# Float32 first-layer weights and x for two blocks, and float32 P and V turned by TensorE for the first

## The chip, the cores and the metric

One core of one Trainium2 chip runs the whole kernel. The metric is the device time of one execution in microseconds; a kernel is run several times and the median counts.

## What is computed

Attention over 4 batches, 8 heads, 576 positions and a head width of 64, with q and k rotated by position first, then two dense layers over the 2304 tokens that come out:

```python
q_rot, k_rot = (rotate(q), rotate(k))
scores = scale * np.matmul(q_rot, k_rot.transpose(0, 1, 3, 2))
attn = np.exp(scores - np.max(scores, axis=-1, keepdims=True))
attn = attn / (np.sum(attn, axis=-1, keepdims=True) + 1e-09)
x = np.matmul(attn, v)                     # to (2304, 512)
h = x @ w_in                               # (512, 2048)
g = np.maximum(h, 0.0) + alpha * np.minimum(h, 0.0)
out = g @ w_out                            # (2048, 512)
```

## The kernel before, in words

The tokens are 18 tiles of 128, two to a block, nine blocks. A batch has 4.5 tiles, so tiles 4 and 13 hold the end of one batch and the start of the next and are worked in halves (`half_pair`). Heads go in pairs: of each tile and pair of heads, `pair` has PE multiply q with k in float32 (L655; a half tile L683), and `head` then has DVE find the maximum (L707), ACT take the exponential with its sum (L716), ACT or DVE write 16 P as float16 (L721), DVE write what that leaves as a second float16 (L735), and SP turn both parts by one DMA transpose (L739). PE multiplies the turned parts with V (L746), which `values` holds as two float16 parts too; the low part of the first batch is made by PE (L467, L468) and copied by ACT (L471). After a tile's last pair `normalise` divides by the sums (y, L761), splits y into two float16 parts (L765 or L766, L768), and a DMA transpose makes x (xt, L775).

`expert` works a block's 16 slots, one for each 128 columns of w_in. The first layer is 12 float16 matmuls of 256 columns in two halves (L789: high by high, high by low, low by high), the activation is one ACT and one DVE instruction (L800, L803), and the second layer adds into a PSUM bank pair over all slots: for blocks 0 and 1 (`NF` = 2) as two float32 matmuls of 512 columns (L809), for the rest as six in a reduced float32 with g and w_out in two parts each (L827). `result` scales by a power of two on ACT (L839) and stores.

The weights come as raw float64 and are converted by three DVE instructions for each 128 x 512 chunk (`to_f32`, L508, L513, L517). `weights` does this for four groups, each of four chunks of w_in and four of w_out. For w_in ACT takes the absolute maximum (L538), a chain of small DVE instructions and one PE matmul makes a power-of-two scale (L542, L366 to L368, L354), and then ACT (L582) and DVE (L586) write two float16 parts; a w_out chunk is scaled by ACT (L599). `split` cuts w_out in two in block 1 for the blocks after it (L609, L613).

Block 0's attention runs first, alone, with the loads and the first weights. Then block 0's slots run beside block 1's attention and the other three groups of weights; block 1's slots run beside block 2's attention, and so on. The order on each engine's queue is written out ahead of time: every operation has a priority (`at`, the slot in which it is wanted, less a lead from `PRM`) and prices in ns for the engines that may take it, and `Plan.run` goes through a model of the five engines, giving a free engine its most urgent ready operation. On the chip each engine works through its queue in order. In the plan DVE and POOL share a port. Three PSUM bank pairs (`pair_T`) hold scores in block 0's attention; SP issues all loads, stores and transposes.

## Time and profile before

| | |
|---|---|
| median of 3 runs | 688.65 us (685.98 to 691.06) |
| profiled execution | 684.13 us |
| its span in the profile | 682.3 us |
| PE busy | 608.4 us, 89% |
| DVE busy | 507.9 us, 74% |
| ACT busy | 339.9 us, 50% |
| POOL busy | 181.0 us, 27% |

PE is TensorE's matmuls, PEld its weight loads, DVE VectorE, ACT ScalarE, POOL GpSimd, SP SyncE. Ends of matmuls are modelled in the profile, so a price of PE is best read from the start of one group to the start of the next. A float32 matmul stands in the trace as two instructions. The granted clock is a share of 2.4 GHz; 0.5 is 1.2 GHz.

### The profile page before, as it was taken

The page shows a single profiled execution, that of the slowest core. Times are in us where ns is not written, and L with a number is a line of the kernel's source. Part 1 is how long each engine was busy: PE and PEld are TensorE (multiplying, and loading weights), DVE is VectorE, ACT ScalarE, POOL GpSimd, SP SyncE. Part 2 cuts the span into 40 slices and gives each one's busy share as a digit, 9 for nine tenths or more (in the row PEclk, how much of TensorE's full clock was granted, in tenths as well). Part 3 has the DMA queues.
Part 4 walks back from the last instruction along what each step waited for, and adds up shares of the span by engine and source line. Part 5 has one row for each costly group of instructions (what it writes and reads, how often), then busy time and mean ns, then how long its engine had stood idle before and what let it go on. Part 6 is the DMA issues. An engine that isn't in the chain of part 4 may idle for free.

```text
span 682.3 us, 13828 instructions
## 1 busy us (share of the span) xinstructions
PE 608.4 (89%) x5384; PEld 443.8 (65%) x5384; DVE 507.9 (74%) x879; ACT 339.9 (50%) x766; POOL 181.0 (27%) x145
## 2 busy tenths in 40 slices
PE   0656678779899999999999999999999999999997
PEld 0334444455656567777767777677777777777775
DVE  5998999999778776768886586777866667765332
ACT  3536747539743435545654545464545445543322
POOL 4763000204642212126623222253211202110000
PEclk9966669979999999999999999999999999999999
DMA  8999898695985745468896456774445555462000
GB/s 302 312 233 226 159 292 214 193 272 121 222 167 108 135 86 132 86 114 184 198 211 106 99 118 103 112 183 100 84 69 105 110 78 86 101 119 54 32 0 32
DMA packets 209009, 96.47 MB, mean 141 GB/s; under 512 B 191792, under 2 KB 196016, under 8 KB 208944
## 3 DMA queue, kind: packets, MB, share of 16 engines
q1 hardware_dynamic: 208944, 95.59, 63.0%
q8 instruction: 42, 0.69, 0.4%
q14 instruction: 23, 0.19, 0.1%
HBM read 41.56 MB, written 4.72 MB: 68 GB/s over the span
## 4 chain that ended last, share of the span: by engine, by line
PE 68%; DMA 18%; DVE 10%; issue 1%; ACT 1%; SPq 1%; POOL 0%; ACTq 0%; DVEq 0%; POOLq 0%
PE h L789 24%; PE pair L827 21%; DMA pt<-pp 14%; PE v L746 8%; PE pair L655 8%; PE pair L809 5%; PE pair L683 2%; DVE kraw L390 1%; DMA qr<-in_q_dram 1%; DMA kraw<-in_k_dram 1%; DVE pp L735 1%; DVE mx L707 1%; DVE wi L586 1%; DMA wraw<-in_moe_w_out_dram 1%; DVE wraw L517 1%
## 5 line engine op out<-in xcount | busy, mean ns | idle before, releaser
L789 PE MATMUL h<-xt,wi 128*128 128x256 f16 x1728 | 231.4, 277 | 11.1 <-DVE r L803 10.6
L789 PEld LDWEIGHTS <-wi 128*128 128x128 f16 x1728 | 156.3, 99 | 72.3 <-issue 53.5
L716 ACT ACTIVATE e<-pair,mx 128x576 f32<-128x576 f32 x144 | 105.6, 736 | 87.7 <-DVE mx L707 83.5
L735 DVE SCALAR_TENSOR_TENSOR pp<-e,pp 128x576 f16<-128x576 f32 x144 | 126.1, 882 | 8.1 <-ACT pp L721 7.0
L803 DVE SCALAR_TENSOR_TENSOR r<-r,beta,h 128x256 f32<-128x256 f32 x144 | 68.7, 477 | 75.9 <-ACT r L800 75.6
L800 ACT ACTIVATE r<-h 128x256 f32<-128x256 f32 x144 | 55.1, 383 | 132.4 <-PE h L789 129.5
L746 PE MATMUL v<-vv,pt 128*128 128x64 f16 (+1 forms) x2240 | 92.6, 199 | 30.1 <-DMA pt<-pp 29.8
L746 PEld LDWEIGHTS <-pt 128*128 128x128 f16 (+1 forms) x2240 | 84.0, 104 | 51.3 <-DMA pt<-pp 41.6
L707 DVE TENSOR_REDUCE mx<-pair 128x1 f32<-128x576 f32 x144 | 103.2, 750 | 11.7 <-PE pair L655 10.3
L827 PE MATMUL pair<-wh,gh 128*128 128x512 f32 x224 | 96.0, 429 | 0.7 <-ACT gh L817 0.7
L655 PE MATMUL pair<-ks,qn 64*128 64x288 f32 x512 | 89.4, 453 | 7.2 <-ACT e L716 6.2
L827 PE MATMUL pair<-wh,gl 128*128 128x512 f32 x224 | 87.6, 391 | 0.8 <-POOL gl L820 0.8
L827 PE MATMUL pair<-wo,gh 128*128 128x512 f32 x224 | 88.2, 394 | 0.0
L820 POOL TENSOR_TENSOR gl<-r,gh 128x256 fp32r<-128x256 f32 x49 | 48.3, 986 | 116.5 <-ACT gh L817 80.1
L655 PEld LDWEIGHTS pair<-ks,qn 64*128 64x128 f32 x512 | 48.8, 196 | 35.5 <-issue 12.5
L721 ACT ACTIVATE pp<-e 128x576 f16<-128x576 f32 x90 | 61.1, 681 | 15.8 <-DMA pt<-pp 14.8
L817 ACT ACTIVATE gh<-r 128x256 fp32r<-128x256 f32 x97 | 40.4, 416 | 51.0 <-PE pair L827 33.9
L809 PE MATMUL pair<-wo,r 128*128 128x512 f32 x128 | 61.7, 607 | 0.0
L768 POOL TENSOR_TENSOR xs<-y,xs 128x512 f16<-128x512 f32 (+1 forms) x19 | 27.8, 1463 | 109.9 <-DVE xs L766 85.9
L827 PEld LDWEIGHTS pair<-wh,gl 128*128 128x128 f32 x224 | 42.0, 188 | 11.2 <-POOL gl L820 1.6
L827 PEld LDWEIGHTS pair<-wh,gh 128*128 128x128 f32 x224 | 42.2, 189 | 10.1 <-issue 1.9
L820 DVE TENSOR_TENSOR gl<-r,gh 128x256 fp32r<-128x256 f32 x63 | 28.7, 456 | 26.2 <-ACT gh L817 25.5
(77 smaller groups left out, 555.3 us busy)
## 6 DMA issues: line engine op xcount, KB each, us to landing
kraw<-in_k_dram SPq DMA_DIRECT2D x16, 576.0 KB, 4.6
qr<-in_q_dram SPq DMA_DIRECT2D x18, 512.0 KB, 4.2
wraw<-in_moe_w_in_dram SPq DMA_DIRECT2D x16, 512.0 KB, 5.5
wraw<-in_moe_w_out_dram SPq DMA_DIRECT2D x16, 512.0 KB, 5.6
vraw<-in_v_dram SPq DMA_DIRECT2D x16, 320.0 KB, 4.4
out_dram<-os SPq DMA_DIRECT2D x18, 256.0 KB, 2.2
pt<-pp SPq DMA_TRANSPOSE x144, 3.4
vv<-vv SPq DMA_DIRECT2D x32, 64.0 KB, 2.2
```

The source lines that it names most:

```text
L655: nc.tensor.matmul(out=ps[h]()[:, x, :HS], lhsT=qn()[r, p], rhs=kt()[r, x * HS:(x + 1) * HS], start=True, stop=True)
L707: lambda e: nc.vector.tensor_reduce(out=mx()[a:z], in_=ps()[a:z, :, :HS], axis=AX.XY, op=ALU.max, negate=True),
L716: lambda e: nc.scalar.activation(out=ex()[a:z].rearrange("p (x c) -> p x c", x=2), in_=ps()[a:z, :, :HS], func=ACTF.Exp, bias=mx()[a:z], a ...
L721: lambda e: nc.scalar.activation(out=pp()[a:z, 0], in_=ex()[a:z], func=ACTF.Copy, scale=1.0 if early else E_SC) if e == ACT
L735: lambda e: nc.vector.scalar_tensor_tensor(out=pp()[a:z, 1], in0=ex()[a:z], scalar=E_SC, in1=pp()[a:z, 0], op0=ALU.mult, op1=ALU.subtract),
L746: nc.tensor.matmul(out=v_b()[c:d, 2 * p + g], lhsT=pt()[:, s, o:o + d - c], rhs=vt()[:, g, w], start=(n == 0), stop=(n == len(order) - 1))
L789: nc.tensor.matmul(out=ps(), lhsT=wi_b()[:, kk, j // FG, w, f], rhs=x()[:, y * KC + kk], start=(kk == 0 and n == 0), stop=(kk == KC - 1 an ...
L800: lambda e: nc.scalar.activation(out=g(), in_=ps(), func=ACTF.Relu, scale=-1.0),
L803: lambda e: nc.vector.scalar_tensor_tensor(out=g(), in0=g(), scalar=beta_b()[:, j:j + 1], in1=ps(), op0=ALU.mult, op1=ALU.add),
L809: nc.tensor.matmul(out=po()[:, x], lhsT=g()[:, x * 128:(x + 1) * 128], rhs=wf[j](), start=(j == 0), stop=(j == KF - 1))
L820: lambda e: ENG[e].tensor_tensor(out=gl(), in0=g(), in1=gh().bitcast(F32), op=ALU.subtract),
L827: nc.tensor.matmul(out=po()[:, x], lhsT=s()[:, ts], rhs=w, start=(j == 0 and c == 0), stop=(j == KF - 1 and c == 2))
```

## The change

- `weights` only converts now, two chunks in one instruction (`load_two`, `to_f32` on 1024 elements), in place, and keeps the absolute maxima; w_in stands in SBUF as float32.
- Blocks 0 and 1 do the first layer with four float32 matmuls of 256 columns (`l1_f32`) on a float32 x, which `normalise` makes for tiles 0 to 3 by four matmuls of y against the identity and a copy out of PSUM.
- In block 1's slots one scale for all of w_in is made (`bound_w_in`), and after each group's last slot `split_in` writes the two float16 parts over the float32 ones, for blocks 2 to 8. w_out isn't scaled any more; `result` multiplies by the scale from block 2 on.
- For tiles 0 and 1, `head_f32` takes the place of the second half of `head`: five float32 matmuls of 128 columns of the exponentials against the identity, into the PSUM tile that held the scores, one copy to SBUF on ACT or DVE, and five float32 matmuls of 64 columns with the raw V. V's scale is multiplied into the reciprocal sums instead.
- `PRM`, the leads of all operations, has new values throughout; for instance keys lead by 23.6 and not 40.87, batch 0's V by 40.33 and not 32.45, units look ahead by 3 and not 2. Prices of the plan change: DVE's fixed part from 68 to 130 ns, a small DVE instruction from 75 to 150, the DMA rate from 360 to 340, two halves of the first layer for blocks 0 and 1 at 860 instead of 655.
- The attention of block 1 no longer interleaves with `weights` in program order, which matters only between equal priorities.

```diff
+    def load_two(at, g, src):
+        raw, token = wr_T.new(), flow.new()
+        for x in range(2):
+            op(at, {SP: t_dma(128 * 512 * 8)},
+               lambda e, x=x: nc.sync.dma_start(out=raw()[:, x].rearrange("p f w -> p (f w)").bitcast(I64), in_=src(x)),
+               writes=[(raw, x), token])
+        return raw, token
+
+    def w32(c, g):
+        return wi_b().bitcast(F32)[:, c, g].rearrange("p a b -> p (a b)")
 
     def weights(g):
         at = slot(0, FG * g)
-        wm, m, ps = wm_T.new(), column(at - 8), pair_T[1 + g % 2].new()
-        raws = []
+        for c in range(0, KC, 2):
+            raw, token = load_two(at - PRM["wl"] + PRM["wg"] * g, g, lambda x, c=c: w_in[c + x, g])
+            two = lambda c=c: wi_b().bitcast(F32)[:, c:c + 2, g].rearrange("p c a b -> p c (a b)")
+            ti, acc = lambda two=two: two().bitcast(I32), [(wi_b, (c, g)), (wi_b, (c + 1, g))]
+            to_f32(at - PRM["wb"], raw, ti, acc, ti, acc, token)
+            op(at - PRM["ws"], {ACT: t_act(1024, ap=1)},
+               lambda e, raw=raw, c=c, two=two: nc.scalar.activation(
+                   out=raw().bitcast(F32)[:, :, :, 1], in_=two(), func=ACTF.Abs, accum_out=wmax_b()[:, c // 2, g:g + 1]),
+               reads=acc, writes=[(raw, 0), (raw, 1), (wmax_b, (c, g))])
+        for n in range(g * FG // 2, (g + 1) * FG // 2):
+            w = new_wf(n)
+            wf[n] = w
+            at = slot(0, 2 * n)
+            raw, token = load_two(at - PRM["wl2"] + PRM["wg"] * g, g, lambda x, n=n: w_out[2 * n + x])
+            ti = lambda w=w: w().bitcast(I32)
+            to_f32(at - PRM["wb2"], raw, ti, [w], ti, [w], token)
...
+    def split_in(g):
+        at = slot(NF, FG * g) - PRM["si"]
         for c in range(KC):
-            raw, token = wr_T.new(), flow.new()
-            raws.append((raw, token))
-            op(at - PRM.get('wl', 16) + PRM.get('wg', 2) * g, {SP: t_dma(128 * 512 * 8)},
-               lambda e, raw=raw, c=c: nc.sync.dma_start(
-                   out=raw().rearrange("p f w -> p (f w)").bitcast(I64), in_=w_in[c, g]),
-               writes=[raw, token])
-        for c, (raw, token) in enumerate(raws):
-            tmp = lambda c=c: wi_b().bitcast(I32)[:, c, g]
-            dst = lambda raw=raw: raw()[:, :, 1]
-            to_f32(at - PRM.get('wb', 5), raw, tmp, (wi_b, (c, g)), dst, raw, token)
-            op(at - PRM.get('wb', 5), {ACT: t_act(512, ap=1)},
-               lambda e, raw=raw, c=c, tmp=tmp: nc.scalar.activation(
-                   out=tmp().bitcast(F32), in_=raw().bitcast(F32)[:, :, 1], func=ACTF.Abs,
-                   accum_out=wm()[:, c:c + 1]),
-               reads=[raw], writes=[(wi_b, (c, g)), (wm, c)])
-        op(at - 4, {DVE: 80}, lambda e: nc.vector.tensor_reduce(out=m()[:, 0:1], in_=wm(), axis=AX.X, op=ALU.max),
-           reads=[(wm, c) for c in range(KC)], writes=[m], port=False)
-        bound(at - 4, m, lambda: we_b()[:, g:g + 1], (we_b, g), ps)
-        we, wsc, wus = (lambda b=b: b()[:, g:g + 1] for b in (we_b, wsc_b, wus_b))
-        scale_of(at - 4, wsc, (wsc_b, g), we, (we_b, g))
-        small(at - 4, lambda: scalar(wus(), we(), 2.0**-14, None, ALU.mult), reads=[(we_b, g)], writes=[(wus_b, g)])
-        by_pe = g < PRM["wpe"]
-        if by_pe:
-            dg = diagonal(at - 4, wsc, (wsc_b, g))
-        for c, (raw, _) in enumerate(raws):
-            f = lambda raw=raw: raw().bitcast(F32)[:, :, 1]
-            t = lambda c=c: wi_b()[:, c, g]
-            acc = (wi_b, (c, g))
-            if by_pe:
-                op(at - PRM['ws'], {ACT: t_act(512, ap=1)},
-                   lambda e, f=f, t=t: nc.scalar.activation(
-                       out=t()[:, 0], in_=f(), func=ACTF.Copy, scale=wsc_b()[:, g:g + 1]),
-                   reads=[raw, (wsc_b, g)], writes=[acc])
-                if c % 2:
-                    ps = pair_T[1 + g % 2].new()
-                    last = raws[c - 1][0]
-                    low_part(at - PRM['ws'], dg, ps,
-                             lambda ps=ps, c=c, rs=(last, raw): [
-                                 (ps()[:, x], rs[x]().bitcast(F32)[:, :, 1], wi_b()[:, c - 1 + x, g, 0]) for x in range(2)],
-                             lambda ps=ps, c=c: (wi_b()[:, c - 1:c + 1, g, 1], ps()),
-                             [last, raw, (wi_b, (c - 1, g))], [(wi_b, (c - 1, g)), acc], 1024)
-                continue
-            if c >= PRM["fi"]:
-                op(at - PRM.get('ws', 3), {ACT: t_act(512, ap=1)},
-                   lambda e, f=f: nc.scalar.activation(out=f(), in_=f(), func=ACTF.Copy, scale=wsc_b()[:, g:g + 1]),
-                   reads=[(wsc_b, g)], writes=[raw])
-                op(at - PRM.get('ws', 3), {ACT: t_act(512), DVE: (t_dve(512, fast=True), PRM.get('wh', 4))},
-                   lambda e, f=f, t=t: nc.scalar.activation(out=t()[:, 0], in_=f(), func=ACTF.Copy) if e == ACT
-                   else nc.vector.tensor_copy(out=t()[:, 0], in_=f()),
-                   reads=[raw], writes=[acc])
-                op(at - PRM.get('ws', 3), {POOL: t_pool(512, True), DVE: (t_dve(512), PRM.get('wlo', 0))},
-                   lambda e, f=f, t=t: ENG[e].tensor_tensor(out=t()[:, 1], in0=f(), in1=t()[:, 0], op=ALU.subtract),
-                   reads=[raw], writes=[acc])
-                continue
-            op(at - PRM.get('ws', 3), {ACT: t_act(512, ap=1)},
-               lambda e, f=f, t=t: nc.scalar.activation(
-                   out=t()[:, 0], in_=f(), func=ACTF.Copy, scale=wsc_b()[:, g:g + 1]),
-               reads=[raw, (wsc_b, g)], writes=[acc])
-            op(at - PRM.get('ws', 3), {DVE: t_dve(512, 1)},
-               lambda e, f=f, t=t: nc.vector.scalar_tensor_tensor(
-                   out=t()[:, 1], in0=f(), scalar=wsc_b()[:, g:g + 1], in1=t()[:, 0], op0=ALU.mult, op1=ALU.subtract),
-               reads=[raw, (wsc_b, g)], writes=[acc])
-        for j in range(g * FG, (g + 1) * FG):
-            raw, token, w = wr_T.new(), flow.new(), new_wf(j)
-            wf[j] = w
-            at = slot(0, j)
-            op(at - PRM.get('wl2', 14) + PRM.get('wg', 2) * g, {SP: t_dma(128 * 512 * 8)},
-               lambda e, raw=raw, j=j: nc.sync.dma_start(out=raw().rearrange("p f w -> p (f w)").bitcast(I64), in_=w_out[j]),
-               writes=[raw, token])
-            ti = lambda w=w: w().bitcast(I32)
-            to_f32(at - PRM.get('wb2', 3), raw, ti, w, ti, w, token)
-            op(at - PRM['ws2'], {ACT: t_act(512, ap=1)},
-               lambda e, w=w: nc.scalar.activation(out=w(), in_=w(), func=ACTF.Copy, scale=wus_b()[:, g:g + 1]),
-               reads=[(wus_b, g)], writes=[w])
+            tmp, acc, t = os_T.new(), (wi_b, (c, g)), lambda c=c: wi_b()[:, c, g]
+            op(at, {ACT: t_act(512, ap=1), DVE: (t_dve(512, fast=True), PRM["sd"])},
+               lambda e, c=c, tmp=tmp: nc.scalar.activation(out=tmp(), in_=w32(c, g), func=ACTF.Copy, scale=wsc_b())
+               if e == ACT else scalar(tmp(), w32(c, g), wsc_b(), None, ALU.mult),
+               reads=[acc, wsc_b], writes=[tmp])
+            op(at, {ACT: t_act(512), DVE: (t_dve(512, fast=True), PRM["sd"])},
+               lambda e, t=t, tmp=tmp: nc.scalar.activation(out=t()[:, 0], in_=tmp(), func=ACTF.Copy) if e == ACT
+               else nc.vector.tensor_copy(out=t()[:, 0], in_=tmp()),
+               reads=[tmp], writes=[acc])
...
+            op(at, {POOL: t_pool(512, True), DVE: (t_dve(512), PRM["wlo"])},
+               lambda e, t=t, tmp=tmp: ENG[e].tensor_tensor(out=t()[:, 1], in0=tmp(), in1=t()[:, 0], op=ALU.subtract),
+               reads=[tmp], writes=[acc])
...
+        if t < PRM["pf"]:
+            return head_f32(at, t, b, p, h, ex, ps, pt)
+        pp = pp_T.new()
...
+    def head_f32(at, t, b, p, h, ex, ps, pt):
+        v_b, raw = vos[t], vraw[b, p]
+        pt.make = lambda: pt_T.pool.tile([128, NH, 128], F32, name="pt", tag=f"pt{pt_T.opened % pt_T.bufs}")
+        flat = lambda: ps().rearrange("p x c -> p (x c)")
+
+        def turn(e):
+            for s in range(NH):
+                w = min(128, S - 128 * s)
+                nc.tensor.matmul(out=flat()[:w, 128 * s:128 * s + 128], lhsT=ex()[:, 128 * s:128 * s + w],
+                                 rhs=eye_b(), start=True, stop=True)
+
+        def pv(e):
+            for s in range(NH):
+                w = min(128, S - 128 * s)
+                nc.tensor.matmul(out=v_b()[:, 2 * p + h], lhsT=pt()[:w, s], rhs=raw()[:w, h, s],
+                                 start=(s == 0), stop=(s == NH - 1))
+
+        op(at + 0.3, {PE: 1300}, turn, kind=WIDE, reads=[ex, eye_b], writes=[ps])
+        op(at + 0.3, {ACT: t_act(NH * 128, True), DVE: (t_dve(NH * 128), PRM["pc"])},
+           lambda e: nc.scalar.activation(out=pt().rearrange("p s c -> p (s c)"), in_=flat()[:, :NH * 128], func=ACTF.Copy) if e == ACT
+           else nc.vector.tensor_copy(out=pt().rearrange("p s c -> p (s c)"), in_=flat()[:, :NH * 128]),
+           reads=[ps], writes=[pt], port=False)
+        op(at + 0.6, {PE: 1000}, pv, kind=WIDE, reads=[pt, raw], writes=[(v_b, (2 * p + h, 0))])
...
+        if t < PRM["pf"]:
+            small(at, lambda: scalar(r(), r(), vs[b]()[a:z], None, ALU.mult), reads=[vs[b]], writes=[rs])
...
+        if t < 2 * NF:
+            i, o = divmod(t, 2)
+            if i not in xt:
+                xt[i] = xt_T.new()
+                xt[i].make = lambda: xt_T.pool.tile([128, KC, 256], F32, name="xt", tag=f"xt{xt_T.opened % xt_T.bufs}")
+            yf, vf = lambda: y().rearrange("p h d -> p (h d)"), lambda: vo().rearrange("p h d -> p (h d)")
+
+            def turn(e):
+                for c in range(KC):
+                    w = slice(128 * c, 128 * c + 128)
+                    nc.tensor.matmul(out=vf()[:, w], lhsT=yf()[:, w], rhs=eye_b(), start=True, stop=True)
+
+            op(at, {PE: 1100}, turn, kind=WIDE, reads=[(y, a), eye_b], writes=[(vo, (h, a)) for h in range(H)])
+            op(at, {ACT: t_act(DM, True), DVE: (t_dve(DM), 2)},
+               lambda e: (nc.scalar.copy if e == ACT else nc.vector.tensor_copy)(
+                   out=xt[i]()[:, :, o * 128:(o + 1) * 128], in_=vf().rearrange("p (c n) -> p c n", c=KC)),
+               reads=[(vo, (h, a)) for h in range(H)], writes=[(xt[i], o)], port=False)
+            return
...
+        def l1_f32(e, half):
+            f = slice(j % FG * 128, (j % FG + 1) * 128)
+            for kk in range(half * KC // 2, (half + 1) * KC // 2):
+                nc.tensor.matmul(out=ps(), lhsT=w32(kk, j // FG)[:, f], rhs=x()[:, kk], start=(kk == 0), stop=(kk == KC - 1))
...
-            op(at, {PE: 655}, lambda e, half=half: l1(e, half), kind=HALF * half,
+            op(at, {PE: 860 if i < NF else 655}, lambda e, half=half: (l1_f32 if i < NF else l1)(e, half), kind=HALF * half,
...
+                if j == 0:
+                    bound_w_in()
+                if j % FG == FG - 1 and j < KF - 1:
+                    split_in(j // FG)
         result(i, po)
+        if i == NF - 1:
```

## Rows read from the trace of the kernel before

**Rows 1.** The page's 40 slices of the span (17 us each), in tenths.
```profile
PE   0656678779899999999999999999999999999997
...
DVE  5998999999778776768886586777866667765332
...
PEclk9966669979999999999999999999999999999999
```

**Rows 2.** Windows by stage: busy us of each engine, granted clock, DMA share, GB/s.
```profile
core 0: us, PE busy (x) PEld busy (x) DVE busy (x) ACT busy (x) POOL busy (x), PEclk, DMA share, GB/s
20.00:85.20 65.20, 41.25 (x342) 26.48 (x340) 59.77 (x84) 37.45 (x77) 28.63 (x16) 0.69 0.95 228
85.20:184.10 98.90, 80.21 (x593) 49.02 (x593) 94.19 (x181) 63.17 (x135) 23.32 (x18) 0.89 0.82 214
184.10:262.00 77.90, 75.28 (x680) 48.91 (x679) 60.22 (x96) 33.42 (x73) 22.58 (x16) 1.00 0.62 128
```

**Rows 3.** The chain that ended last, stage A: start us, us, what.
```profile
31.64 7.67 DMA pt<-pp
...
42.57 7.55 DMA pt<-pp x2
...
53.09 5.07 DMA pt<-pp
...
60.66 9.33 DMA pt<-pp x2
```

**Rows 4.** PE's timeline, full clock: start us, us, line, operation, count.
```profile
152.18 0.28 PE L368 MATMUL pair<-cr,ones 128*128 128x1 f32 x2
152.32 0.57 PE L746 MATMUL v<-vv,pt 128*128 128x64 f16 x14
152.72 0.82 PE L789 MATMUL h<-xt,wi 128*128 128x256 f16 x6
153.47 1.24 PE L655 MATMUL pair<-ks,qn 64*128 64x288 f32 x8
154.65 0.83 PE L789 MATMUL h<-xt,wi 128*128 128x256 f16 x6
...
164.11 2.19 PE L683 MATMUL pair<-ks,qd 128*128 128x288 f32 x8
166.13 1.47 PE L789 MATMUL h<-xt,wi 128*128 128x256 f16 x12
167.44 1.88 PE L809 MATMUL pair<-wo,r 128*128 128x512 f32 x4
169.16 0.57 PE L746 MATMUL v<-vv,pt 128*128 128x64 f16 x14
```

**Rows 5.** Groups by line, whole span, then PE in stage A: busy us, mean ns.
```profile
L683 PEld LDWEIGHTS pair<-ks,qd 128*128 128x128 f32 x64 | 11.6, 190 | 3.3 <-issue 0.7 <-ACT xs L765 0.2
...
L471 ACT ACTIVATE vv<-pair 128x640 f16<-128x640 f32 x4 | 2.8, 703 | 5.9 <-PE pair L468 5.9
...
L467 PE MATMUL pair<-vraw,dg 128*128 128x320 f32 x14 | 5.7, 499 | 1.6 <-ACT vv L471 1.6
```

**Rows 6.** DVE's groups by line in stage A, the last in stage M0.
```profile
L735 DVE SCALAR_TENSOR_TENSOR pp<-e,pp 128x576 f16<-128x576 f32 x18 | 17.2, 963 | 2.3 <-ACT pp L721 2.3
...
L354 DVE TENSOR_SCALAR pp<-e 128x576 f16<-128x576 f32 x2 | 4.7, 2348 | 0.7 <-DMA pt<-pp 0.7
...
L586 DVE SCALAR_TENSOR_TENSOR wi<-wraw,wsc,wi 128x512 f16<-128x512 f32 x4 | 3.7, 965 | 0.0
...
L354 DVE TENSOR_SCALAR wus<-we 128x1 f32<-128x1 f32 x1 | 0.1, 142 | 0.0
...
L586 DVE SCALAR_TENSOR_TENSOR wi<-wraw,wsc,wi 128x512 f16<-128x512 f32 x13 | 10.5, 818 | 0.0
```

**Rows 7.** Timelines of DVE and PE between block 0's last y and its first slot.
```profile
78.67 0.68 DVE L761 TENSOR_TENSOR y<-v,rs 128x512 f32<-128x512 f32 x1
...
85.17 2.72 PE L789 MATMUL h<-xt,wi 128*128 128x256 f16 x12 [0.23 <-DMA xt<-xs]
```

More of the change, by code (lines that the diff above doesn't have):

```diff
@@ L617, in attention_moe @@
+           reads=[f, (h, j % 4)], writes=[(l, y)])
     qs = {}
@@ L907, in attention_moe @@
         result(i, po[i])
+    if NF == NB:
+        raise ValueError("the second block comes with float32 weights")
     for i in range(NB, len(blocks)):
```

157 lines of the change are left out of this document (86 added, 71 removed).

## The prediction

> **What bounds the kernel now.** I read the page's slices first [rows 1]: from about 190 us on PE is in its highest tenth and at full clock in nearly every slice, so what is left to win there is work, not waiting; before that PE is mostly at six to eight tenths, while DVE stands at nine. Next the stages [rows 2], cut where the PE timeline shows block 0's attention, block 0's expert layers and block 1's expert layers to begin and end. From 20 to 85.2 us (call it A: block 0's attention, first weights) DVE is busy 59.8 of 65.2 us, the DMA engines 95%, PE only 41.3 us and at a granted clock of 0.69, so part of that is half speed (1.2 and not 2.4 GHz). From 85.2 to 184.1 us (M0: block 0's 16 slots, block 1's attention, three quarters of the weights) DVE is busy 94.2 of 98.9 us, PE 80.2 at 0.89. From 184.1 to 262 us (M1: block 1's slots) PE is busy 75.3 of 77.9 at 1.00 and DVE 60.2. A and M0 are bound by DVE and, in A, by transposes; M1 and all that follows by PE. The chain of A says which wait ends last there [rows 3]: four pieces of it, 29.6 us together, are six DMA transposes of P, 4.9 us each with the queue before them, and PE sits idle until they land.
>
> **The change part by part.** All PE prices are start to start at full clock, from one stretch [rows 4]: QK of a pair 1.18 us (153.47 to 154.65), P times V of one head in float16 0.40 (14 matmuls, 152.32 to 152.72), the first layer of a slot in float16 1.31 (166.13 to 167.44), the second in float32 1.72 (167.44 to 169.16).
>
> *First layer in float32, 32 slots.* 12 float16 matmuls of 256 columns become 4 float32 ones of 256. The second layer has 2 float32 matmuls of 512, the same number of columns, at 1.72; so the first costs 1.72 and not 1.31, 0.41 more, 6.6 us for each of the two blocks. M1 is PE's already, so there it is paid in full; in M0 it is paid only if PE has become the bound.
>
> *P in float32, 16 heads.* A head loses the float16 copy, DVE's subtraction and a DMA transpose with SP's issue, and gains on PE 5 float32 matmuls of 128 columns (P against the identity), a copy of 640 elements out of PSUM, and 5 float32 matmuls of 64 columns (P times V). The trace writes a float32 matmul as two instructions. The one of 288 columns takes 2.02 us for 8 (164.11 to 166.13 in [rows 4]), 253 ns, 0.88 ns a column; so the turning is 10 x 112 ns = 1.12 us. For 64 columns that price would be 56 ns, but a weight load goes with each: the one-column matmul with its float32 load, twice, keeps PE 0.14 us (152.18 to 152.32 in [rows 4]), 70 ns each. So P times V is 0.70, a head 1.82 instead of 0.40, and 16 heads 29.1 instead of 6.4: 22.7 us more. Bounds: by columns alone a head is 1.68 (2.2 us less in all); if each of the 20 loads held PE for its whole 190 ns [rows 5] it would be 3.8 (31.7 us more). I take 1.82, because in [rows 4] the loads of equal kind hide behind their matmuls.
>
> The Trainium skill (TensorE: Matmul & The Clock Gate, sections LDWEIGHTS (loading the stationary operand) and Weight-path perf modes) speaks against this: a load costs the stationary operand's columns over 1.2 in ns, 107 for 128, and the fast load is not to be had with float32. By it, as an estimate, P times V would be 10 x 107 ns, a head 2.2 us and the 16 heads 6 us dearer than my sum, which rival (b) covers; the trace's 70 ns for load and matmul together is under that.
>
> The copy out of PSUM goes to ACT or DVE; a 640 wide one on ACT takes 0.70 us [rows 5], what the float16 copy of P took there, so ACT gains nothing and loses nothing. DVE loses in A the subtraction, 16 of the 18 for 17.2 us, 15.3, and the two copies it made for 4.7 [rows 6].
>
> *x in float32, 4 tiles.* Split, subtraction on POOL and transpose go; 4 float32 matmuls of 128 columns (8 x 112 ns, 0.9 us) and a copy of 512 come. From y to the first layer it took 6.5 us (78.67 to 85.17) [rows 7]; now about 0.7 + 0.9 + 0.7 and the handovers, some 2.5. Four microseconds less at the start of M0, 3.6 us more PE over both blocks.
>
> *Weights.* Group by group, w_in is no longer scaled and split before block 0's first layer: the subtractions of L586, 3.7 us of DVE in A and 10.5 in M0, go, and so do the bound and scale chains, about a dozen small instructions a group, 1 us in A and 3 in M0. Converting 1024 at a time makes 48 instructions of 96; what that saves no row shows by itself, and it lies between nothing and 48 times the 0.14 us of a whole one-column instruction [rows 6], 7 us. I take 3 over A and M0, 2.5 of it in M0. The scaling of w_out on ACT goes into the last copy, for nothing. The split of w_in comes back in M1: 16 times two copies and a subtraction, about 1.3 us ACT (or less on DVE) and 1.5 us POOL each. In M1 ACT is busy 33.4 and POOL 22.6 of 77.9 us [rows 2], which covers 21 and 24 us. If it did not, block 2's first slots would be late by what is missing, at most a few us; its bound needs one PE matmul with a DVE chain of under 1 us.
>
> *SP and DMA.* 16 transposes of P and 4 of x leave SP's queue; the loads behind them (L530, L594, q) go out earlier. The loads keep their bytes. V is loaded ahead of K now; the first QK waits for K and q in either order, so I leave 20 us as the start.
>
> *The sum.* A after: V's low part some 5 us of PE at full clock (its float32 half in A is 5.7 us busy, partly cold [rows 5], and the float16 half beside it is smaller), QK 8 x 1.18 = 9.4, heads 29.1, two turns of x 1.8: 45 us. DVE's is 59.8 - 15.3 - 4.7 - 3.7 - 1 = 35. PE is now the longer of the two. What clock? In A, PE was cold with idle gaps from P's transposes in its queue; those gaps go, the work per pair triples, and at half clock PE would have no idle time at all, the condition in which the trace shows 1.00 (M1). So I take full clock. PSUM lets little more than one pair be in flight: QK, maximum, exponential, turning, copy of a first head are 1.2 + 0.75 + 0.75 + 1.1 + 0.7 and four handovers, about 5.4 us, against 4.8 of PE work in a pair. That is 85 to 88%. So A takes 45 / 0.85 = 53 us, and M0 starts at about 75 and not 85.2. M0 after: 16 x (1.72 + 1.72) = 55, six QK 7.1, half pairs 4.9, P times V 8, two turns 1.8, and two pairs of block 1 that stood in A before, 3.2: 80 us. DVE: 94.2 - 10.5 - 3 - 2.5 and 5 for those pairs, 83. Two engines near 80 leave neither free; at the 95% that DVE had, 88 us. M0 ends at 163 and not 184.1: 21 us won. M1 gives 6.6 back. Net 14.5: the profiled execution (span 682.3, 684.1 with what lies around it) becomes about 669.6, 2.1% less, and the median of the runs, 688.65, about 674.
>
> **Rivals.** (a) *The gain is whole*: A and M0 dense on PE at 95%, 125 us from 20, M0 ends at 152; net 25, 663. For it speaks that M1 runs at 97%; against it that DVE needs 83 us in M0 by itself. (b) *Nothing comes of it*: the heads cost 2.3 us (the planner's own prices in the diff, 1300 and 1000), 8 us more, and PE, whose queue is in order, waits at each turning for an exponential that DVE's conversions have delayed, so A keeps its end near 83. Then M0 ends at 171 to 177 and net it is 0 to 7: 682 to 689. For it speaks that DVE's instructions in A are drawn out beside a busy POOL (963 ns for a subtraction, 2348 for a copy of P [rows 6]) and might stay so. (c) *Slower*: the clock stays low in A. 45 us of PE work at 0.5 with no gap are 90, so M0 starts at 110 and ends near 198, net 21 the other way, 709. It decides from a granted clock under some 0.6 in A; there the 0.69 of before would give 45 / 0.69 / 0.85 = 77, M0 from 99 and a loss of about 10, 699. For it speaks only that A was cold; against it that it was cold beside idle PE. (d) That the split of w_in doesn't fit beside M1 is a mishap of a few us within (b).
>
> **How the numbers follow.** About 1% (7 us) is what a measurement of this kernel can tell from no change. The forecast, 7 to 21 us won, has 0.48, its own range 667 to 682; (a) 0.15; (b) 0.21; (c) 0.16. So faster 0.63, within 1% 0.21, slower 0.16. The range reaches from (a) with cheap heads, 655, to the milder half of (c) and the dear heads, 697; beyond it lie the rest of (c) and a little of (a).
>
> **What would show it.** In the changed profile: no P transposes ahead of M0; granted clock in A near 1; first-layer float32 slots at 1.72 us; a turning of 10 instructions at 1.1 and P times V at 0.7; first L1 of block 0 near 75 us and block 0's last second layer near 163; M1 about 6 us longer than 77.9 at 1.00; DVE in A well under nine tenths. Wrong if: the clock of A stays near 0.69, loads make the heads 3 us, PE's gaps wait for DVE or ACT before turnings, or the later, PE-bound part (from 262 us on), which I leave at its length, moves by more than 3 us through the new priorities.

## The result and the profile after

The changed kernel takes 678.33 us in the median of 4 runs (675.64 to 680.75), the kernel before 689.38 beside it (4 runs). The ratio is 0.9851, 95% interval 0.9818 to 0.9883: 1.5% faster, 10 to 11 us. The prediction said 674.0, range 655 to 697, and the forecast's own range 667 to 682 holds the median. The profiled run took 676.41 us, span 674.6, against 684.13 and 682.3. The time is right; the way there is not the one predicted. Stage times come from the one traced execution of each kernel, which for `b_pf2`, `b_newprm`, `a_pad`, `a_l1h1` and `o_late` is the slowest of its runs and for `a_l1h0` the fastest. Cut at block 0's first slot and at the ends of the two blocks' second layers, as in [rows 2] (the last column is the time behind 262 us before, behind 253.1 us after):

| | A ends at | M0 | M1 | behind M1 |
|---|---|---|---|---|
| before | 85.2 | 98.9 | 77.9 | 420.3 |
| predicted | 75 | 88 | 84.5 | 420.3 |
| after | 88.4 | 83.6 | 81.1 | 421.5 |
| after less before | +3.2 | -15.3 | +3.2 | +1.2 |

A should have given 10 us and cost 3; M0 gave more than was asked of it, and M1 took half of what was feared. The sum is -7.7 us in the two profiled runs; the medians differ by 11, as the profiled run of before (684.13) lies 5 us under its kernel's median.

The page's 40 slices of after (17 us each, tenths), to be read beside [rows 1]:

```profile
PE   1998999999999999999989999999999999999997
...
DVE  4889799875877767587759776777766665664332
...
PEclk9999999999999999999979999999999999999999
```

PE is in its two highest tenths and, but for one slice, at full clock from the second slice on, in A too, where it stood at six to eight tenths and 0.69 before. The windows of after for A, M0 and M1, columns as in [rows 2]:

```profile
core 0: us, PE busy (x) PEld busy (x) DVE busy (x) ACT busy (x) POOL busy (x), PEclk, DMA share, GB/s
21.70:88.40 66.70, 60.82 (x421) 48.53 (x420) 55.88 (x61) 30.92 (x61) 31.13 (x17) 1.00 0.69 249
88.40:172.00 83.60, 83.47 (x597) 56.40 (x598) 65.94 (x101) 47.50 (x102) 13.87 (x12) 1.00 0.74 161
172.00:253.10 81.10, 80.50 (x582) 53.03 (x581) 61.84 (x102) 45.62 (x94) 46.64 (x30) 1.00 0.57 127
```

A is PE's now: 60.8 of 66.7 us, where 45 were forecast. In M0 DVE fell from 94.2 to 65.9 us and PE is busy all the time.

The chain that ended last, in A, one pair of heads from turning to turning (start us, us, what), and under it PE's timeline of the same pair and of three groups of M0 (start us, us modelled, line, operation, count):

```profile
34.18 2.97 PE pair L745 x20
37.15 1.28 PE v L751 x9
38.43 1.19 PE pair L638 x8
39.63 0.75 DVE mx L690
40.46 0.62 ACT e L699
```

```profile
34.18 2.97 PE L745 MATMUL pair<-eye,e 128*128 128x128 f32 x20 [0.38 <-ACT e L699]
37.08 1.35 PE L751 MATMUL v<-vraw,pt 128*128 128x64 f32 x9
38.13 0.51 PE L638 MATMUL pair<-ks,qn 64*128 64x288 f32 x1
38.27 0.27 PE L751 MATMUL v<-vraw,pt 64*128 64x64 f32 x1
38.39 1.19 PE L638 MATMUL pair<-ks,qn 64*128 64x288 f32 x7
39.50 1.47 PE L751 MATMUL v<-vraw,pt 128*128 128x64 f32 x10
41.34 2.97 PE L745 MATMUL pair<-eye,e 128*128 128x128 f32 x20 [0.38 <-ACT e L699]
...
91.50 1.99 PE L817 MATMUL h<-xt,wi 128*128 128x256 f32 x8
93.33 1.88 PE L843 MATMUL pair<-wo,r 128*128 128x512 f32 x4
95.05 0.98 PE L727 MATMUL v<-vv,pt 128*128 128x64 f16 x28
```

The chain of [rows 3], with its DMA transposes of P, is gone. In its place stands a cycle of 7.16 us a pair (34.18 to 41.34): two turnings 2.90 (to 37.08), P times V of one head 1.31 (to 38.39), QK 1.1 to 1.2, P times V of the other 1.46, 0.38 idle. So a head costs (2.90 + 1.31 + 1.46) / 2 = 2.84 us, not 1.82. A first layer of block 0 takes 1.83 (91.50 to 93.33).

DVE's conversions in A of after, by line (busy us, mean ns):

```profile
L516 DVE SCALAR_TENSOR_TENSOR wi<-wraw,wi 128x1024 int32<-128x1024 int32 x5 | 8.2, 1633 | 0.0
L511 DVE TENSOR_SCALAR wi<-wraw 128x1024 int32<-128x1024 int32 x5 | 6.5, 1292 | 0.3 <-DMA wraw<-in_moe_w_in_dram 0.3
L511 DVE TENSOR_SCALAR wo<-wraw 128x1024 int32<-128x1024 int32 x4 | 5.3, 1337 | 0.0
```

Nine pairs of chunks, 18 of the 32, are begun by DVE in A. Before it was 8 chunks. So part of what DVE no longer does for P, it spends on weights ahead of time. In M0 its conversions take 24.5 us and not 45.6 (sums of their groups by line), and w_in's subtraction, 10.5 us [rows 6], is gone: that is where M0's 65.9 comes from. How little of it needs the heads, `a_pf0` below shows.

### The profile page after: what moved, and what is told of

Same layout as the page of the kernel before. It is cut to its first block, busy times and chain, and to the rows that moved or that the text cites. A ratio compares the mean times of both kernels' runs of the same rounds, so it can differ in the third digit from the quotient of the medians.

```text
span 674.6 us, 13695 instructions
## 1 busy us (share of the span) xinstructions
PE 643.3 (95%) x5378; PEld 480.3 (71%) x5378; DVE 471.6 (70%) x754; ACT 338.5 (50%) x752; POOL 218.7 (32%) x178
## 4 chain that ended last, share of the span: by engine, by line
PE 85%; DMA 7%; DVE 4%; ACT 2%; issue 1%; SPq 1%; POOL 0%; ACTq 0%; DVEq 0%
PE pair L861 22%; PE h L823 21%; PE pair L638 10%; PE v L727 8%; PE h L817 8%; PE pair L843 7%; DMA pt<-pp 4%; PE pair L745 3%; PE v L751 2%; DMA kraw<-in_k_dram 2%; PE pair L666 2%; PE pair L468 1%; DVE mx L690 1%; DMA qr<-in_q_dram 1%; DMA xt<-xs 1%
## 5 line engine op out<-in xcount | busy, mean ns | idle before, releaser
L823 PE MATMUL h<-xt,wi 128*128 128x256 f16 x1344 | 175.7, 275 | 1.1 <-DMA xt<-xs 0.7
L823 PEld LDWEIGHTS <-wi 128*128 128x128 f16 x1344 | 120.1, 98 | 43.0 <-issue 28.5
L837 DVE SCALAR_TENSOR_TENSOR r<-r,beta,h 128x256 f32<-128x256 f32 x144 | 68.8, 478 | 94.1 <-ACT r L834 93.0
L854 POOL TENSOR_TENSOR gl<-r,gh 128x256 fp32r<-128x256 f32 x69 | 56.4, 818 | 175.6 <-ACT gh L851 152.9
L716 DVE SCALAR_TENSOR_TENSOR pp<-e,pp 128x576 f16<-128x576 f32 x128 | 102.6, 811 | 11.2 <-ACT pp L707 9.5
L727 PEld LDWEIGHTS <-pt 128*128 128x128 f16 (+1 forms) x2016 | 71.9, 102 | 23.0 <-issue 12.3
L727 PE MATMUL v<-vv,pt 128*128 128x64 f16 (+1 forms) x2016 | 78.1, 195 | 4.6 <-DMA pt<-pp 4.6
L638 PE MATMUL pair<-ks,qn 64*128 64x288 f32 x512 | 82.3, 433 | 0.0
L817 PE MATMUL h<-xt,wi 128*128 128x256 f32 x256 | 66.7, 392 | 1.3 <-DVE xt L788 1.2
L817 PEld LDWEIGHTS h<-xt,wi 128*128 128x128 f32 x256 | 45.7, 190 | 14.9 <-issue 5.4
L707 ACT ACTIVATE pp<-e 128x576 f16<-128x576 f32 x76 | 51.4, 679 | 1.0
```

Of the source, the lines that this page charges most:

```text
L638: nc.tensor.matmul(out=ps[h]()[:, x, :HS], lhsT=qn()[r, p], rhs=kt()[r, x * HS:(x + 1) * HS], start=True, stop=True)
L716: lambda e: nc.vector.scalar_tensor_tensor(out=pp()[a:z, 1], in0=ex()[a:z], scalar=E_SC, in1=pp()[a:z, 0], op0=ALU.mult, op1=ALU.subtract),
L727: nc.tensor.matmul(out=v_b()[c:d, 2 * p + g], lhsT=pt()[:, s, o:o + d - c], rhs=vt()[:, g, w], start=(n == 0), stop=(n == len(order) - 1))
L817: nc.tensor.matmul(out=ps(), lhsT=w32(kk, j // FG)[:, f], rhs=x()[:, kk], start=(kk == 0), stop=(kk == KC - 1))
L823: nc.tensor.matmul(out=ps(), lhsT=wi_b()[:, kk, j // FG, w, f], rhs=x()[:, y * KC + kk], start=(kk == 0 and n == 0), stop=(kk == KC - 1 an ...
L837: lambda e: nc.vector.scalar_tensor_tensor(out=g(), in0=g(), scalar=beta_b()[:, j:j + 1], in1=ps(), op0=ALU.mult, op1=ALU.add),
```

## The experiments

Each ratio is to the kernel before, beside which it ran. The stages are named as above.

**Which part carries the gain.** First, the heads of block 0 in float16 again, all else as changed (`a_pf0`):

```diff
-PRM = {"pf": 2, "pc": 3.0, ...
+PRM = {"pf": 0, "pc": 3.0, ...
```

> The changed kernel with P of block 0 again as two float16 parts turned by DMA (pf 0); everything else of the change stays. Theory H (the heads matter): the float32 heads are what took the DMA waits and half of DVE's work out of block 0's attention, so that weights were converted there and the clock stayed full; without them the granted clock before the first slot falls back to about 0.7, the first slot comes at 85 to 90 us, only 8 to 12 of 32 chunks are converted by then, and the kernel is at least 5 us slower than the changed one (ratio to before 0.992 or more). Theory W (the weights matter): the heads cost PE 42 us and gave that stage nothing, as it ends at 88.4 and not 85.2; what was won is w_in's split leaving the stage of block 0's slots, so this kernel is as fast as the changed one or up to 5 us faster (ratio 0.977 to 0.987).

Measured: 677.98 us, 0.9844 (0.9817 to 0.9872), not to be told from the changed kernel. Its windows, and PE's longest wait in A:

```profile
21.70:92.60 70.90, 48.28 (x369) 31.12 (x369) 63.94 (x71) 33.51 (x69) 28.99 (x17) 0.68 0.96 246
92.60:175.30 82.70, 81.92 (x558) 55.72 (x556) 68.71 (x104) 42.91 (x93) 16.99 (x12) 0.98 0.80 210
175.30:258.40 83.10, 80.82 (x582) 52.97 (x581) 65.94 (x104) 46.04 (x95) 42.47 (x27) 1.00 0.62 124
```

```profile
PE v L727 <- DMA pt<-pp: 13.0, 7, 4.0
```

A is bound as it was before, at 0.68 and waiting for transposes (it ends 7 us later than there), and ends 4 us later than with float32 heads; M0 is short all the same. DVE begins 12 chunks in A here, not 18, and is still busy only 68.7 us in M0: its conversions there take 32.2 us (20 chunks at 1.6 us, before 24 at 1.9), and the subtraction of w_in is gone. So float32 P gains nothing in the whole that shows, and M0's gain doesn't need it. In this trace the 4 us come back behind M1, which ends at 258.4 of a span of 676.4 us, 418.0 and not 421.5 us; nothing was edited there, and the cause stays open. The other way round, the float32 heads alone in the kernel before (`b_pf2`):

```diff
-PRM = {"qd": 7.03, ...
+PRM = {"pf": 2, "pc": 3.0, "qd": 7.03, ...
...
+        if t < PRM["pf"]:
+            return head_f32(at, t, b, p, h, ex, ps, pt)
...
```

> The kernel before with nothing but the float32 heads of tiles 0 and 1 (P turned by PE); x, w_in, the order's parameters as before. Theory H: the first stage keeps the full clock, DVE converts 14 or more chunks in it, the stage of block 0's slots shrinks from 98.9 to about 88 us, and without the dearer first layer in float32 (0.5 us a slot in 32 slots, 16 us) this beats the changed kernel: ratio 0.970 to 0.984. Theory W: the first stage gets 3 us longer or more, the slots' stage stays bound by DVE at over 95 us with w_in's split in it, ratio 0.997 to 1.01.

Measured: 709.15 us, 1.0278 (1.0224 to 1.0333). A and M0:

```profile
20.00:111.70 91.70, 76.98 (x422) 59.82 (x420) 47.10 (x69) 35.83 (x73) 22.10 (x13) 0.81 0.33 111
111.70:219.10 107.40, 84.64 (x625) 51.60 (x624) 97.46 (x185) 64.18 (x138) 24.55 (x19) 0.89 0.79 198
```

M0 has DVE at 97.5 us, as before, and is 107 long: with w_in scaled and split ahead of block 0, M0 stays DVE's. A is far too long, and DVE (47 of 92 us) and DMA (0.33) have little to do in it: PE, at 0.81, waits 14.0 us for exponentials, and DVE's queue in turn waits 31.0 us for PE's scores ahead of the maxima. How much the heads cost can't be read from a run so laid out; that M0 is not helped by them can.

The new priorities alone, on the kernel before (`b_newprm`: `PRM` as in the diff, for all names that both kernels have; the planner's prices, which the change raised too, stay old here and new in `a_oldprm`):

> The kernel before with no part of the change but its new numbers for the priorities (those that both kernels have), so that only the order on the engines and queues is new. Theory W (the gain of the changed kernel is the later scaling and split of w_in, and the priorities only fit it): nothing is won, the stage of block 0's slots stays at 95 to 110 us and VectorE's busy time in it near 94; ratio 1.00 to 1.04. Rival P (the priorities themselves made the gain): that stage falls to 82 to 90 us, ratio 0.98 to 0.99.

Measured: 697.04 us, 1.0134 (1.0113 to 1.0154): slower, with A to 93.7, M0 102.5 and DVE busy 91.1 us in it. And the changed kernel with the old priorities (`a_oldprm`):

> The changed kernel with the old values of all parameters that the kernel before has; only pf, pc, si and sd are new. If the new priorities were part of the gain (theory P), the loads and conversions come later than PE wants them, PE idles in the first 170 us, and half or more of the gain is gone (ratio 0.993 or more). If the parts of the change carry it by themselves, the ratio stays within 0.004 of 0.985.

Measured: 702.68 us, 1.0203 (1.0148 to 1.0258); M0 is 87.8, yet A lasts to 110.2, PE waiting 12.3 us for exponentials up to 106 us and its clock at 0.86. Neither the edit without its order nor the order without its edit gains. What the edit does besides the heads (the later split of w_in, the float32 first layer and x, conversions of two chunks at a time) makes M0 short wherever it stands (83 to 88 us in four such kernels against 99 to 107 in three without), and the order decides whether A takes it away again. No run takes these parts of the edit from each other; that the later split is the main one is argued from DVE's rows alone.

**What a head costs.** All 128 wide loads step at 0.11 us; the fifth piece of P is 64 wide. First the piece was filled up with zeros by an operation of its own (`a_pad`):

```diff
...
-                w = min(128, S - 128 * s)
+                w = 128
...
+        op(at + 0.05, {POOL: 200, DVE: (75, 1)}, lambda e: ENG[e].memset(ex()[:, S:640], 0.0), writes=[(ex, "z")])
...
```

> The changed kernel with the exponentials' buffer 640 wide, its last 64 columns set to zero by POOL, so that all five matmuls of a turning and of P times V have 128x128 weights. Theory S: the last chunk's smaller weights break the run of loads hidden behind matmuls; with equal shapes every step is 0.11 us, a turning 1.1 and not 1.4 us, P times V 1.1 and not 1.2, 0.4 us a head, and as block 0's attention is bound by PE, 16 heads give 5 to 6.5 us: first slot at about 82 us, ratio to before 0.975 to 0.979. Theory L: the gaps are waits for the exponentials or handovers that stay whatever the shape, or DVE ends the stage anyway; ratio unchanged within 0.003 of 0.985.

Measured: 700.43 us, 1.0164 (1.0108 to 1.0219), first slot at 106.1. The new operation had changed the whole written-out order; PE waited 18.1 us for exponentials and ran at 0.84 in A. This decides nothing on the loads. So the order was held fixed: in `a_wide` the last piece is columns 448 to 575, 128 wide and with 128 rows (it then doesn't match V's rows, so this kernel serves only to compare the work), in `a_pad2` 64 zeros are written behind P by ScalarE inside the exponential's own operation.

```diff
-                w = min(128, S - 128 * s)
+                w = 128
...
-lhsT=ex()[:, 128 * s:128 * s + w]
+lhsT=ex()[:, min(128 * s, S - 128):][:, :128]
...
```

> The changed kernel with every instruction in the same order, but the last of the five pieces of P (keys 512 to 575) turned as the 128 columns 448 to 575 and multiplied as 128 rows, so that all ten weight loads of a head have one shape. Its keys are then counted wrongly, so the output differs; the work is the same or more. Theory S (a narrower last piece breaks the run of loads, 0.45 to 0.55 us a head): turning 1.1 us, P times V 1.1, so 16 heads take 7 to 8.5 us less of TensorE; the first slot comes at 80 to 83 us in place of 88.4 and, since TensorE was the bound from there on, the whole is 5 to 8 us shorter, ratio to the kernel before 0.973 to 0.978. Rival L (the gaps come from the handovers between heads): nothing moves, 88 us and 0.985. Rival D (the heads do get shorter, but the weights for the first slots are not converted or loaded earlier): first slot at 82, gain given back in the 16 slots, 0.982 to 0.985.

> As a_wide, but right: e is 640 wide and ScalarE writes 64 zeros behind P after each exponential of the first two tiles (16 more small ScalarE instructions of some 0.2 us, 3 us of its idle time); the order of all other instructions is that of the changed kernel. Theory S: as a_wide or up to 1 us longer, ratio 0.973 to 0.98. Rival Z (the zeros stand in the chain exponential, turning and lengthen it by 0.2 us a head): A gains only 4 us, ratio 0.978 to 0.982. Rival L: 0.985.

Measured: `a_wide` 680.47 us, 0.9869 (0.9809 to 0.9929), `a_pad2` 681.84, 0.9899 (0.9845 to 0.9953); first slots at 89.5 and 90.1. PE's timeline in `a_wide`, and DVE's and POOL's in the same stretch:

```profile
56.12 2.40 PE L745 MATMUL pair<-eye,e 128*128 128x128 f32 x20
58.35 1.23 PE L751 MATMUL v<-vraw,pt 128*128 128x64 f32 x10
59.51 1.24 PE L638 MATMUL pair<-ks,qn 64*128 64x288 f32 x8
60.68 1.33 PE L751 MATMUL v<-vraw,pt 128*128 128x64 f32 x10
65.83 4.63 PE L745 MATMUL pair<-eye,e 128*128 128x128 f32 x20 [3.83 <-ACT e L699]
```

```profile
59.06 3.63 DVE L516 SCALAR_TENSOR_TENSOR wo<-wraw,wo 128x1024 int32<-128x1024 int32 x1
62.62 1.21 DVE L520 SCALAR_TENSOR_TENSOR wi<-wraw,wi 128x1024 int32<-128x1024 int32 x1
63.75 1.41 DVE L690 TENSOR_REDUCE mx<-pair 128x1 f32<-128x576 f32 x2
...
58.02 3.60 POOL L390 TENSOR_TENSOR kraw<-kraw,tab 128x1152 f32<-128x1152 f32 x1
```

```profile
62.00:66.00 4.00, 0.17 (x2) 0.17 (x2) 4.00 (x5) 2.14 (x5) 0.00 (x0) 0.79 0.28 82
66.00:72.00 6.00, 6.00 (x32) 5.93 (x34) 3.98 (x5) 1.91 (x4) 0.00 (x0) 0.57 0.65 206
```

On the load the theory holds: two turnings take 2.23 us (56.12 to 58.35) and not 2.90, P times V 1.16 and not 1.31, a head about 2.3 and not 2.84. On the time it fails. The faster PE reaches this turning sooner, but its exponential needs a maximum that stands in DVE's queue behind two conversions, one of them 3.63 us long beside POOL's multiplication of the keys (1.21 us alone). On ScalarE the exponential also stands behind the Abs of w_in (its absolute maxima), which needs the second conversion and runs from 63.86 to 64.97, half a microsecond past the first maximum's end. PE stands 3.83 us, and the clock is 0.57 in the next 6 us. Much of what the loads gave is lost at this place.

**Is it that place?** The same maxima were moved in the written-out order: one 1.21 us conversion more ahead of them in the changed kernel (`o_late`), and two conversions fewer ahead of them, in `a_pad2` (`a_first`) and in the changed kernel (`o_first`). In the last two the Abs that needs these conversions moves behind the exponentials with them; all three also hold the small tile `dg` in another buffer.

```diff
 DVE, o_late                             DVE, a_first and o_first
+SCALAR_TENSOR_TENSOR wo<-wraw,wo        +TENSOR_REDUCE mx<-pair (twice)
 TENSOR_REDUCE mx<-pair (twice)           SCALAR_TENSOR_TENSOR wo<-wraw,wo
-SCALAR_TENSOR_TENSOR wo<-wraw,wo         SCALAR_TENSOR_TENSOR wi<-wraw,wi
                                         -TENSOR_REDUCE mx<-pair (twice)
```

> The changed kernel with one 1.21 us conversion more ahead of the same two maxima on VectorE, no other edit. Theory V (TensorE's wait there is set by VectorE's queue, and past it the clock falls): the wait grows by 1.2 us or a little more, the granted clock falls to 0.5 for some 10 us behind it, the first slot comes at 93 to 96 us and the whole is 5 to 8 us over the changed kernel, ratio 0.992 to 0.998. Rival N (nothing rests on that place): first slot at 88 to 90, ratio 0.985 to 0.988.

> a_pad2 (the last piece of P 128 wide) with one change of order, in one place: the two maxima of the sixth pair of block 0 stand ahead of two weight conversions on VectorE, and the two exponentials ahead of the Abs on ScalarE that needs those conversions; everything else in the order of the changed kernel. Theory V (in a_pad2 TensorE got through its heads faster and then stood 4.0 us before 66.1 us, because the maxima were queued behind a conversion that took 3.64 us beside a busy GpSimd, and the clock fell to half after it, some 4 us more): the gap shrinks to about 1 us, the clock stays at 1.00 through A, the first slot comes at 81 to 84 us and not 90, and the whole is 4 to 8 us under a_pad2, ratio to the kernel before 0.978 to 0.983. Rival N (another stall takes its place, or the weights hold the first slots): first slot 87 or later, ratio 0.985 to 0.99.

> The changed kernel (last piece of P 64 wide) with the same one change of order as a_first. Theory V: in the changed kernel the wait there was 1.1 us in the profiled run, and the clock held in that run but not in the run with half of block 1's first layer, whose first 90 us are the same program; with the maxima ahead, it holds in every run: first slot 86 to 88 us, ratio 0.981 to 0.985, no runs near 681. Rival N: as the changed kernel or slower, 0.985 to 0.99.

Measured: `o_late` 684.51 us, 0.9965 (0.9932 to 0.9997), first slot at 96.4; `a_first` 678.09, 0.9841 (0.9806 to 0.9877), 86.9; `o_first` 680.30, 0.9893 (0.9853 to 0.9932), 89.4. From `o_late`, PE's row of the timeline at the place, and the window behind it:

```profile
67.18 4.25 PE L763 MATMUL pair<-eye,e 128*128 128x128 f32 x20 [2.36 <-ACT e L716]
```

```profile
68.00:80.00 12.00, 12.00 (x50) 9.79 (x50) 6.44 (x8) 2.96 (x6) 0.00 (x0) 0.52 0.36 118
```

With one instruction of 1.21 us more in front of the maxima PE waits 2.36 us, where the changed kernel's longest such wait was 1.1, the clock is 0.52 for the next 12 us, and the kernel is slower, 0.9965 against 0.9851, intervals apart: the place counts in that direction, as expected. It is the ten runs that show it. The trace alone would not: the order of the changed kernel also gave a first slot at 94.1 once (`a_l1h1`, below), and 5 us of the 691.09 us of `o_late`'s traced execution are lost in M1, 85.9 us long (see below). In the other direction it doesn't pay. From `a_first`, PE's row of the timeline and ScalarE's:

```profile
65.57 1.33 PE L776 MATMUL v<-vraw,pt 128*128 128x64 f32 x10 [1.37 <-ACT pt L781]
...
63.69 1.16 ACT L566 ACTIVATE wraw<-wi 128x1024 f32<-128x1024 f32 x1 [1.02 <-DVE wi L542]
...
64.81 1.30 ACT L781 ACTIVATE pt<-pair 128x640 f32<-128x640 f32 x2
```

The wait for the exponential is 0.5 us now, but the Abs of w_in, moved back with its conversions, holds the copies of the turned P, and PE waits 1.37 us for those instead; from 66 to 80 us the clock is 0.76. `a_first` wins 3.2 us of A against `a_pad2` and ends level with the changed kernel; `o_first` wins none. No version here beats the changed kernel by more than its interval.

**Is M0, is M1 PE's alone?** Two of the four float32 matmuls of the first layer were left out, in block 0's slots (`a_l1h0`, `i == 0`) or in block 1's (`a_l1h1`, shown), same order; this takes 0.8 to 0.9 us of PE from each of 16 slots, 13 to 15 us.

```diff
-            for kk in range(half * KC // 2, (half + 1) * KC // 2):
+            for kk in [half * 3] if i == 1 else range(half * KC // 2, (half + 1) * KC // 2):
```

> The changed kernel in the same order, with two of the four float32 matmuls of the first layer left out in block 0's 16 slots (output differs). Theory E (in block 0's slots TensorE is now the bound, as its 83.5 us busy of 83.6 say): the stage 83.6 us less 14 to 15, ratio 0.963 to 0.966. Rival D (weights, converted by VectorE, 65.9 us of work, and carried by the DMA engines, 0.74 busy, hold it as they did before): TensorE waits for them and the stage shrinks by 3 to 8 us, ratio 0.974 to 0.981.

> The changed kernel in the same order, with two of the four float32 matmuls of the first layer left out in block 1's 16 slots (output differs). Theory E (block 1's slots are bound by TensorE, each float32 matmul of 256 columns is paid in full at some 0.45 us): that stage 81.1 us less 14 to 15, the whole 14 to 15 us shorter, ratio 0.963 to 0.966. Rival Q (the split of w_in and w_out on ScalarE, GpSimd and VectorE has to be done in that stage and holds it): the stage shrinks by 5 us or less, or block 2's first slots wait; ratio 0.976 or above.

Measured: `a_l1h0` 676.83 us, 0.9835 (0.9769 to 0.9901), `a_l1h1` 680.60, 0.9872 (0.9809 to 0.9935). M0 of `a_l1h0` is 78.0 us and not 83.6; M1 of `a_l1h1` is 82.6 and not 81.1. The window of that M1 and PE's waits in it:

```profile
176.90:259.50 82.60, 72.51 (x522) 42.38 (x521) 66.25 (x107) 45.29 (x94) 49.31 (x30) 0.96 0.62 129
```

```profile
PE v L727 <- DMA pt<-pp: 5.8, 6, 3.0
PE h L368 <- DVE r L837: 3.5, 1, 3.5
```

Theory E falls in both, in the medians too. With less for PE to do, M0 gives back 6 of the 13 to 15 us and M1 nothing against the changed kernel. P's transposes for the next block's attention are right behind PE (3.5 us of waits in that M0, 5.8 in that M1), in M1 DVE too (3.5), and the clock there is 0.96 where it was 1.00. But DVE's 3.5 us are not of this edit. They stand before the matmul of w_in's bound at the start of M1, where DVE is held in two copies of 64 x 4 elements beside three multiplications of POOL on end (172.55 to 180.83). The copies in `a_l1h1`, and in the changed kernel:

```profile
175.98 4.88 DVE L673 COPY sums<-st 64x4 f32<-64x4 f32 x2
...
168.88 0.34 DVE L673 COPY sums<-st 64x4 f32<-64x4 f32 x2
```

Two kernels with the whole first layer show the same: the copies take 4.90 us in `o_first` and 4.87 in `o_late`, PE waits 2.8 and 2.7 us, the clock is 0.60 and 0.57 in the 4 us behind, and M1 lasts 85.6 and 85.9 us. Five traces without that wait or with 0.3 us of it (the changed kernel, `a_wide`, `a_pad2`, `a_first`, `a_l1h0`) have an M1 of 80.8 to 82.3. So in M1 the edit gave nothing against the latter, some 3 us against the former. A stage with PE at 99% was not a stage that PE alone sets.

`a_l1h1` shows something else. Up to 88 us it is the changed kernel's program, yet its first slot came at 94.1. Its windows at the place:

```profile
62.00:66.00 4.00, 2.50 (x19) 2.17 (x18) 3.98 (x5) 2.64 (x6) 0.00 (x0) 1.00 0.28 82
66.00:80.00 14.00, 14.00 (x57) 11.45 (x57) 8.10 (x9) 3.67 (x7) 0.00 (x0) 0.51 0.56 178
```

PE was busy 2.50 of the 4 us before 66, with a wait of 1.5 us for an exponential (2.92 and 1.1 in the profiled run of the changed kernel), and after that at 0.51 for 14 us, where the changed kernel had 1.00. So that kernel stands at the edge there, and one execution was 6 us later than another at the first slot. What tipped it is not shown.

## Why the prediction was right, and where it was not

**Heads (term mis-sized, the largest miss).** 1.82 us a head was forecast, 2.84 came: 16 x 1.02 = 16.3 us of PE, about the difference between the 60.8 us that PE is busy in A and the 45 of the sum, and more than the 13.4 us by which A ended late. Two steps of it failed. P times V was priced at 70 ns an instruction by a one-column matmul, of which I took load and matmul together; that price doesn't hold for a stream of instructions that each bring a new load. In `a_wide` ten instructions of 64 columns take 1.16 us, 116 ns each, nearly the same as those of 128 columns (2.23 / 20 = 112). That is the Trainium skill's rule (TensorE: Matmul & The Clock Gate, section LDWEIGHTS (loading the stationary operand)), by which 128 columns of weights take an estimated 107 ns and which the prediction had set aside. This trace agrees with it, at 112 to 116. And "the loads of equal kind hide behind their matmuls" missed that the last piece is not of equal kind: it costs 0.3 us a turning and 0.15 or more each P times V. The 2.84 is inside the bounds given (1.68 to 3.8).

**A's bound.** PE is A's bound and the clock is full, both as said. That 85% of PE would do was too low (91%), but A ended at 88.4 and not 75, later than before. (The sum's own figures give 73, 20 + 53, and 89%, 4.8 of 5.4 us, where it says 75 and 85 to 88%; beside the heads that is little.) DVE's 35 us in A became 55.9. Here rival (b) is what happened, with a head of more than its 2.3 us, and M0's end at 172.0 lies in its 171 to 177. PE's waits for exponentials were 3.1 us in all in the changed kernel, and 7.4, 18.1 and 12.3 in `a_wide`, `a_pad` and `a_oldprm`, where A ended later still.

**x by PE.** From y to the first layer 2.5 us were forecast, 6.5 before [rows 7]. DVE's timeline of after:

```profile
85.13 0.69 DVE L771 TENSOR_TENSOR y<-v,rs 128x512 f32<-128x512 f32 x1 [1.68 <-PE v L751]
85.74 0.68 DVE L511 TENSOR_SCALAR wi<-wraw 128x1024 int32<-128x1024 int32 x1
86.34 1.42 DVE L690 TENSOR_REDUCE mx<-pair 128x1 f32<-128x576 f32 x2
87.67 0.68 DVE L788 COPY xt<-v 128x512 f32<-128x512 f32 x1
```

The first slot starts at 88.40, 3.3 us after y: 3.2 saved, not 4, in part because the copy stands behind a conversion and two maxima (PE's turning of y ends at about 87.2).

**Rival (c)** was right about the danger and wrong about the place: the clock does not stay low from the start of A, it falls behind a single stall at 62 to 67 us, and costs some 6 us where it does (12 us at 0.52 in `o_late`).

**M0.** 88 forecast, 83.6 measured. PE's 80 us became 83.5 (a first layer at 1.83 and not 1.72 is 1.8 of that, and a 17th first layer, the first of block 1, another 1.8). DVE's 83 became 65.9: the working took P's copies, w_in's split and the small chains off DVE, but let the conversions lie where they lay. Ten of them moved into A, in part into the time that P had left free there: 18 chunks and not 8 are begun by then, 12 in `a_pf0` where P stays with DVE. So the two engines near 80 that I saw were one, and M0 went at PE's pace, as rival (a) had it. That M0's gain doesn't need the heads, and doesn't come from the priorities alone, is shown by `a_pf0` (M0 82.7 without float32 heads), `b_pf2` (107.4 with the heads alone) and `b_newprm` (102.5 with the priorities alone). That it comes from taking w_in's split out of M0, and not from the wider conversions beside it, is argued: in `a_pf0` DVE's rows give 10.5 us to the subtraction, some 8 to the four chunks begun earlier and some 6 to the cheaper chunk.

**M1.** 6.6 forecast, 3.2 measured. The first layer costs 0.52 more a slot and not 0.41, so by my step M1 should have grown by 8 us. PE's busy time grew by 5.2. The first layers inside M1, before and after:

```profile
L789 PE MATMUL h<-xt,wi 128*128 128x256 f16 x205 | 27.9, 273 | 1.3 <-DVE r L803 1.3
L817 PE MATMUL h<-xt,wi 128*128 128x256 f32 x120 | 32.0, 394 | 0.0
```

120 instructions are 15 slots, with 13 more for block 2's first (L823), where M1 of before had all 16 and one of block 2. The units look ahead by 3 and not 2, and one of block 1's first layers now stands in M0: 1.8 us of the 8. P times V has 28 instructions fewer there, 0.8 us more. And PE's idle time fell from 2.6 to 0.6 us. These three make up 4.6 of the 5 us that are missing. So the step that failed is "there it is paid in full": PE had 2.6 us of M1 free, and the count of 16 slots in M1 didn't hold in the new order. That less work of PE doesn't shorten M1 by as much, `a_l1h1` adds. The split of w_in was hidden, as said: block 2's first layer waited for none of it, and what lies behind M1 grew by 1.2 us.

**Why the total held.** The errors have opposite signs, which is luck: A 13.4 us worse, M0 4.4 and M1 3.4 better, the rest 1.2 worse, 6.8 in all: 669.6 was forecast for the profiled run, 676.4 measured. How much of M0's better part is due to A's being longer (more time to convert in) was not taken apart.

**Left open.** Two of the changed kernel's four runs lie near 676 and two near 680.5; whether the stall in A, or the one at the start of M1, makes that difference is not shown, since only one of the four has a trace.

## What to carry to other kernels

Price a matmul that reloads its weights by the load, not by its columns, and look for the one piece of another shape that breaks the run. When an edit takes work off an engine, ask what that engine will do next in its written-out queue: here the gain came up one stage later than the work that was removed. Where the order is fixed by hand and other engines are close behind, taking work off the busiest need not shorten the stage by as much (6 of 13 to 15 us in M0 here), so test an edit and its order together. And count what falls in a stage again when the order changes: a unit that runs one slot further ahead moves work across the cut.
